# Linear attention into a SoLU block: three of nine chunks take their attention with tokens on partitions

## The chip, the cores and the metric

The kernel runs on one core of a Trainium2 chip. Its engines work beside each other, each through its own instructions in order: TensorE (PE in the profile, its weight loads PEld), VectorE (DVE), ScalarE (ACT), GpSimd (POOL) and SyncE (SP, which here only issues DMAs). They wait for each other by semaphores. The metric is device time in microseconds; lower is better.

## The reference

Inputs are q, k and v of shape (8, 8, 576, 64): batch, heads, tokens, head size; g_norm (64), w_in (512 x 1024), w_out (1024 x 512) and g_ln (1024), all float32.

```
kv  = einsum('bhsd,bhse->bhde', k, v)
out = einsum('bhsd,bhde->bhse', q, kv)
rms = sqrt(mean(out*out, axis=-1) + 1e-6)
x   = (out / rms * g_norm), heads side by side      # 4608 tokens x 512
h   = x @ w_in                                       # 4608 x 1024
sm  = exp(h - max) / (sum(exp(h - max)) + 1e-9)
solu = h * sm
ln  = (solu - mean) / sqrt(var + 1e-6) * g_ln
y   = ln @ w_out                                     # 4608 x 512
```

## The kernel before, in words

The 4608 tokens are nine chunks of 512. Chunks 0 to 7 are one batch each, its tokens j = 0 to 7 of every group of nine; chunk 8 is the ninth token of every group, from all batches. For a chunk c the pieces of work have names, and the prediction uses them:

- `k`, `v`, `q`: loads, converted to bfloat16 on the way, issued on POOL's queue (L265), apart from the first k and v, which SP and ACT issue. `wi`, `wo`: loads of w_in and w_out.
- `kv` (L310): k^T v of a batch; `kc`: its copies to SBUF.
- `qt`/`qc`: q turned by TensorE and copied, in chunks 0 to 4. `qx` (L366): q turned by a DMA, in chunks 5 to 8. `ql`: the ninth tokens put together for chunk 8.
- `o` (L403): q kv, with the features of two heads on partitions and 512 tokens along the row, two banks a piece.
- `sq` (L416, ACT): squares; `s` (L431, TensorE): a matmul with a block matrix of 1/64, which gives the mean of squares of every head to all its 64 partitions; `ln` and `ex` (L435, L439, ACT): its inverse root; `x` (L449, DVE): x = o times that times g_norm.
- `h` (L489 for chunks 0 to 2, L498 for 3 to 8): x w_in; `e` (ACT): exp; `u` (DVE, L523 and L528): h times exp; `r`: squares of u with their sums; in chunks 0 to 2 `g` and `z` add up on POOL and TensorE. `t` (L553): u turned by a DMA that SP issues, in chunks 3 to 8.
- `st`, `rs`: the statistics of the LayerNorm; `a` (L678): u w_out, in halves of four matmuls; `b` (L693, L695): the scaling by the inverse deviation; `d` (L703): the store.
- `wm` (L661), `wc` (L664): the mean of g_ln * w_out over the rows, by TensorE, and w_out centred by it, by DVE. `warm`: matmuls of zeros.
- `gate` (L339): a copy on POOL of one element of the last q, for which all DMA turns wait: no turn starts before the last load has landed.

Nothing is scheduled at run time. `ORDER` is a table with all pieces in one list; the program issues them in that order, and so every engine's order of work, the choice of engine where there is one (`b0.0/act`) and the buffer (`@S0`) are written there. The buffers are slots, of which P (two PSUM banks each, three slots) and S (one bank, two) pace TensorE: a piece that takes a slot waits until the readers of the one before are done. M, L, rst, osq, lss and ob are slots in SBUF. A piece at the head of an engine that waits holds up all that stands behind it there.

```
SLOTS = {"P": 3, "S": 2, "L": 8, "M": 13, "osq": 4, "lss": 3, "rst": 4, "ob": 7}
```

Of the kernel before, what the change touches and what calls it, by code (L numbers as in the profile page):

```python
# [8 lines left out]
FP32 = mybir.dt.float32  # L9
# [15 lines left out]
QUADRANTS = ()  # L25

# [36 lines left out]
WARM = (13, 6, 2, 1)  # L63
# [15 lines left out]
r1.0/pool@L6 qc2.1/dve e1.1@M10 h1.4+@P2 o2.0@P0 sq2.00@osq0 h1.4 sq2.01@osq1 g1.1 h1.5+ h1.5 e1.2@M11 u1.1 u1.2
s2.00@S1 s2.01@S0 ln2.00@lss0 ln2.01@lss1 h1.6+@P1 h1.6 h1.7+ h1.7 a0.20@S1 e1.3@M6 ex2.00@rst0 u1.3 ex2.01@rst1  # L80
o2.1@P2 a0.21 a0.30@S0 sq2.10@osq1 sq2.11@osq0 b0.2/act@ob0 x2.00@M9 x2.01 s2.10@P1 a0.31 s2.11@S1 ln2.10@lss1
ex2.10@rst1 ln2.11@lss0 b0.3/dve@ob2 ex2.11@rst0 qt3.0@P0 qc3.0/dve@M10 kv3@P1 kc3.1/act x2.10 a1.00@S0 a1.01
qt3.1@S1 v6 x2.11 r1.1/pool r1.2/act r1.3/act qc3.1/dve h2.0@P2 h2.1 h2.2@P0 kc3.0/dve e2.0@M1 u2.0@L4 g1.2 g1.3
g2.0@M6 kc3.2/act h2.3 e2.1@M11 u2.1 q6@M12 z1@S1 g2.1 o3.0@P2 sq3.00@osq0 sq3.01@osq1 r2.0/act@L6 r2.1/pool h2.4@P1
y1 st1 rs1 b1.0/dve@ob3 h2.5 h2.6@P0 h2.7 e2.2@M11 u2.2 g2.2 e2.3@M9 a1.10@S1 a1.11 a1.20@S0 u2.3 qt4.0@P1
b1.1/act@ob4 s3.00@S1 g2.3 s3.01@P0 qc4.0/dve@M9 a1.21 b1.2/dve@ob5 r2.2/act r2.3/pool k7@L1 kv4@P1 kc4.1/dve
ln3.00@lss0 ln3.01@lss1 ex3.00@rst0 ex3.01@rst1 x3.00@M11 x3.01 kc4.2/act ql2/pool o3.1@P0 sq3.10@osq1 z2@S1
a1.30@S0 y2 st2 ql5/act v7 q7@M6 gate@L6 s3.10@P2 sq3.11@osq0 ln3.10@lss1 ex3.10@rst1 kc4.0/dve a1.31 x3.10 d0.1/sp
d0.2/sp s3.11@S1 ln3.11@lss0 b1.3/dve@ob0 o4.0@P1 sq4.00@osq0 a2.00@P2 a2.01 ex3.11@rst0 s4.00@S1 a2.10@S0 rs2 x3.11
h3.00@P0 b2.0/dve@ob1 sq4.01@osq1 s4.01@P2 ln4.00@lss0 ex4.00@rst0 ln4.01@lss0 qt4.1@S1 qc4.1/dve x4.00@M2  # L90
ex4.01@rst1 x4.01 h3.01 h3.10@P2 h3.11 e3.0@M10 u3.0@L5 e3.1@M8 u3.1 a2.11 b2.1/act@ob6 kv5@P1 kc5.1/dve r3.0/dve
r3.1/dve o4.1@P0 sq4.10@osq1 d0.3/pool sq4.11@osq0 a2.20@S1 kc5.0/act a2.21 kc5.2/act s4.10@S0 ln4.10@lss0 s4.11@P2
ln4.11@lss1 ex4.10@rst1 ex4.11@rst0 h3.20@P1 h3.21 x4.10 x4.11 e3.2@M8 u3.2 h3.30@P2 h3.31 h4.00@P0 h4.01 h4.10@P1
e3.3@M11 u3.3 r3.2/act t3.0 qx5@M10 ql0/dve e4.0@M9 u4.0@L3 h4.11 e4.1@M0 a2.30@S0 d1.0/pool b2.2/act@ob3 o5.0@P2
sq5.00@osq0 a2.31 sq5.01@osq1 o5.1@P0 sq5.10@osq2 s5.00@S1 u4.1 b2.3/dve@ob2 h4.20@P1 qx6@M1 t3.1 t3.2 ln5.00@lss1
t3.3 t4.0@L4 r3.3/dve st3 sq5.11@osq0 d1.1/sp d1.2/sp d1.3/sp s5.01@S0 d2.0/pool ln5.01@lss0 ex5.00@rst0 x5.00@M11
ex5.01@rst1 s5.10@S1 ln5.10@lss1 x5.01 t4.1 h4.21 a3.00@S0 a3.01 e4.2@M10 u4.2 t4.2 ex5.10@rst1 s5.11@S1 ln5.11@lss0
qx7@M5 x5.10 h4.30@P2 ex5.11@rst0 h4.31 e4.3@M2 a3.10@S1 d2.1/sp x5.11 d2.2/pool kv6@P1 kc6.2/dve a3.11 r4.0/act
h5.00@P0 kc6.0/act kc6.1/dve o6.0@P1 u4.3 rs3 b3.0/dve@ob4 b3.1/act@ob3 sq6.00@osq0 sq6.01@osq2 r4.1/dve h5.01
e5.0@M9 h5.10@P2 s6.00@S0 s6.01@S1 ln6.00@lss0 ln6.01@lss1 ex6.00@rst0 ex6.01@rst1 u5.0@L2 x6.00@M0 x6.01 h5.11  # L100
e5.1@M8 u5.1 a3.20@S0 a3.21 b3.2/dve@ob0 a3.30@S1 r4.2/act r4.3/act o6.1@P1 sq6.10@osq2 kv7@P0 kc7.1/dve a3.31
kc7.0/dve h5.20@P2 h5.21 sq6.11@osq0 b3.3/act@ob5 kc7.2/act st4 d2.3/sp d3.0/sp e5.2@M2 ql4/dve u5.2 s6.10@S1
s6.11@S0 h5.30@P0 h5.31 ln6.10@lss1 ex6.10@rst1 x6.10 ln6.11@lss0 e5.3@M11 a4.00@S1 t4.3 ex6.11@rst1 x6.11 a4.01
a4.10@S0 t5.0@L6 rs4 b4.0/act@ob4 a4.11 b4.1/dve@ob2 o7.0@P2 sq7.00@osq0 sq7.01@osq2 o7.1@P1 a4.20@S1 s7.00@S0 a4.21
# [20 lines left out]
def kernel(  # L125
# [16 lines left out]
    nc = tc.nc  # L142
# [39 lines left out]
    g_cols = big.tile([128, NF + 1], FP32, name="g_cols")  # L182

# [261 lines left out]
    def x_mul(i):  # L445
        c, hf, z = i
        if (hf, z) == (0, 0):
# [210 lines left out]
    def w_mean():  # L658
        t = T["mean"] = bank("mean")
        for f in range(NF):  # L660
            nc.tensor.matmul(t[:, 0], T["g_mean"][:, f, :], T["w_out", f // 4][:, f % 4, :], start=(f == 0), stop=(f == NF - 1))  # L661
# [98 lines left out]
```

## Time and profile before

| | |
|---|---|
| median of 3 runs | 184.74 us (183.53 to 185.95) |
| the profiled execution | 184.59 us |
| span of its instructions | 182.8 us |
| granted TensorE clock, mean | 0.971 |
| busy PE / DVE / ACT / POOL | 167.0 / 123.0 / 136.0 / 61.1 us |
| read from HBM, written to it | 32.51 MB, 9.44 MB |
| DMA queues, share of 16 engines | software (POOL's) 58.1%, hardware (SP's) 36.8% |

Busy times are of one profiled execution. The mean duration of a matmul there (379 ns for 512 columns) counts its whole way through the array; matmuls overlap, and in the chain they follow each other at 0.216 us. The page cuts the span in 40 slices with the busy share in tenths.

### The profile page before, as it was taken

Reading aid. Unit: us, or ns where it says so; the run is one execution under the profiler, and the core shown is the slowest. Engines: PE = TensorE matmul, PEld = TensorE weight load, DVE = VectorE, ACT = ScalarE, POOL = GpSimd, SP = SyncE. Lnnn points to the kernel's source line nnn. Section 1 sums busy time; section 2 is a strip of 40 time slices with the busy share of each in tenths; the row PEclk is TensorE's granted clock in tenths of the full one; section 3 lists DMA queues with packets and bytes.
Section 4 is the critical chain, followed back from the end, with each engine's and each line's share of the span. In section 5 each row is a group of like instructions: output and inputs, shape, how many; then the busy total and the mean of one; then the engine's idle time right before and its main releaser. Section 6 shows DMA issues by size and latency. Waiting matters only on the chain.

```text
span 182.8 us, 4297 instructions
## 1 busy us (share of the span) xinstructions
PE 167.0 (91%) x1719; PEld 82.0 (45%) x1739; DVE 123.0 (67%) x230; ACT 136.0 (74%) x249; POOL 61.1 (33%) x77
## 2 busy tenths in 40 slices
PE   7697977899999999999949999999999999999991
PEld 2342446445455556445413444544444444444450
DVE  1327586866594778678855769757986989765841
ACT  2349765979897878979856999997994787957350
POOL 7851696723695997001310010300000111211020
PEclk9979996999999999999996999999999999999999
DMA  5999999999999999996899999893254999837655
GB/s 172 248 206 280 338 208 209 205 208 212 253 207 232 208 207 208 207 208 105 233 177 221 240 227 227 237 185 71 77 105 71 251 237 209 225 117 157 130 199 203
DMA packets 53591, 36.19 MB, mean 198 GB/s; under 512 B 35580, under 2 KB 48644, under 8 KB 53572
## 3 DMA queue, kind: packets, MB, share of 16 engines
q0 software_dynamic: 15696, 21.17, 58.1%
q1 hardware_dynamic: 37460, 13.90, 36.8%
q10 hardware_dynamic: 416, 0.85, 1.4%
q8 instruction: 13, 0.21, 0.4%
q14 instruction: 6, 0.05, 0.1%
HBM read 32.51 MB, written 9.44 MB: 229 GB/s over the span
## 4 chain that ended last, share of the span: by engine, by line
PE 80%; DMA 8%; DVE 4%; ACT 3%; issue 3%; ACTq 0%; POOLq 0%
PE ps_S L678 27%; PE ps_P L498 21%; PE ps_P L489 11%; PE ps_P L678 6%; DMA sb_M<-sb_M 4%; DMA sb_M<-in_q_dram 4%; PE ps_P L403 3%; PE ps_S L431 3%; PE ps_P L310 3%; DVE sb_M L449 2%; PE ps_S L355 2%; PE ps_P L204 2%; PE ps_S L607 1%; DVE w_out_sb L664 1%; PE ps_P L431 1%
## 5 line engine op out<-in xcount | busy, mean ns | idle before, releaser
L678 PE MATMUL ps_S<-w_out_sb,sb_L 128*128 128x512 bf16 x220 | 54.4, 379 | 1.1 <-issue 0.8
L498 PE MATMUL ps_P<-w_in_sb,sb_M 128*128 128x512 bf16 x190 | 45.2, 385 | 0.2
L678 PEld LDWEIGHTS <-sb_L 128*128 128x128 bf16 x280 | 26.4, 98 | 31.4 <-issue 1.2
L528 DVE SCALAR_TENSOR_TENSOR sb_L<-ps_P,sb_M 128x1024 bf16<-128x1024 f32 x24 | 29.3, 1223 | 11.4 <-ACT sb_M L515 10.9
L703 POOL DMA_DIRECT2D out_dram<-sb_ob x17 | 10.5, 617 | 78.9 <-ACT sb_ob L693 31.2
L449 DVE SCALAR_TENSOR_TENSOR sb_M<-ps_P,g_cols,sb_rst 128x512 bf16<-128x512 f32 x36 | 27.0, 788 | 8.6 <-ACT sb_rst L439 7.4
L515 ACT ACTIVATE sb_M<-ps_P 128x1024 f32<-128x1024 f32 x24 | 24.5, 1022 | 6.9 <-PE ps_P L498 6.7
L498 PEld LDWEIGHTS <-sb_M 128*128 128x128 bf16 x192 | 18.9, 99 | 23.2 <-issue 1.8
L416 ACT ACTIVATE sb_osq<-ps_P 128x512 bf16<-128x512 f32 x36 | 20.0, 595 | 4.7 <-PE ps_P L403 4.6
L489 PE MATMUL ps_P<-sb_M,w_in_sb 128*128 128x512 bf16 x93 | 22.0, 379 | 0.4 <-issue 0.2
L523 DVE TENSOR_TENSOR sb_L<-ps_P,sb_M 128x1024 bf16<-128x1024 f32 x12 | 14.7, 1224 | 8.8 <-ACT sb_M L508 8.6
L439 ACT ACTIVATE sb_rst<-sb_lss 128x512 f32<-128x512 f32 x32 | 19.3, 631 | 0.4
L559 POOL TENSOR_TENSOR sb_M<-sb_M 128x512 bf16<-128x512 f32 x12 | 15.3, 1276 | 4.1 <-issue 2.2
L508 ACT ACTIVATE sb_M<-ps_P 128x1024 f32<-128x1024 f32 x12 | 12.3, 1023 | 4.5 <-PE ps_P L489 4.5
L548 DVE SCALAR_TENSOR_TENSOR sb_M<-sb_L 128x1024 bf16<-128x1024 bf16 x13 | 15.5, 1218 | 0.0
L695 DVE TENSOR_SCALAR sb_ob<-ps_S,rstd 128x512 f32<-128x512 f32 x15 | 11.2, 748 | 6.3 <-PE ps_S L678 5.4
L435 ACT ACTIVATE sb_lss<-ps_S 128x512 f32<-128x512 f32 x23 | 13.4, 594 | 2.0 <-PE ps_S L431 1.9
L489 PEld LDWEIGHTS <-w_in_sb 128*128 128x128 bf16 x96 | 9.0, 97 | 11.5 <-issue 1.8
L693 ACT ACTIVATE sb_ob<-ps_S,rstd 128x512 f32<-128x512 f32 (+1 forms) x15 | 10.1, 671 | 3.7 <-issue 1.8
L546 ACT ACTIVATE sb_M<-sb_L 128x1024 bf16<-128x1024 bf16 x11 | 11.6, 1053 | 1.3 <-DVE sb_L L528 1.3
L431 PE MATMUL ps_S<-sb_osq,head_mean 128*128 128x512 bf16 x26 | 9.9, 407 | 1.3 <-ACT sb_osq L416 1.2
L678 PE MATMUL ps_P<-w_out_sb,sb_L 128*128 128x512 bf16 x47 | 11.0, 379 | 0.1
(85 smaller groups left out, 178.8 us busy)
## 6 DMA issues: line engine op xcount, KB each, us to landing
out_dram<-sb_ob SPq DMA_DIRECT2D x17, 256.0 KB, 3.9
out_dram<-sb_ob POOLq DMA_DIRECT2D x17, 256.0 KB, 4.1
sb_L<-in_k_dram POOLq DMA_DIRECT2D x6, 576.0 KB, 16.4
sb_L<-in_v_dram POOLq DMA_DIRECT2D x6, 576.0 KB, 18.5
sb_M<-in_q_dram POOLq DMA_DIRECT2D x6, 576.0 KB, 17.3
sb_L<-in_moe_w_out_dram POOLq DMA_DIRECT2D x2, 1024.0 KB, 15.5
sb_M<-in_q_dram POOLq DMA_DIRECT2D x4, 288.0 KB, 11.1
w_in_sb<-in_moe_w_in_dram POOLq DMA_DIRECT2D x2, 512.0 KB, 11.1
```

Of the source, the lines that this page charges most:

```text
L416: nc.scalar.activation(out=t[:, :], in_=T["o", c, hf][:, z], func=AF.Square)
L431: nc.tensor.matmul(t[:, 0], head_mean[:, :], T["osq", i][:, :], start=True, stop=True)
L439: nc.scalar.activation(out=t[:, :], in_=T["lss", i][:, :], func=AF.Exp, scale=-0.5)
L449: nc.vector.scalar_tensor_tensor(out=T["x", c][:, pairs_of(c, hf), :, z], in0=T["o", c, hf][:, z].rearrange("p (n q) -> p n q", n=2), scal ...
L489: nc.tensor.matmul(t[:, f % 2], w_in_sb[:, dt, f * 128:(f + 1) * 128], T["x", c][:, dt].rearrange("p q z -> p (q z)"), start=(dt == 0), st ...
L498: nc.tensor.matmul(T["h", c, m][:, half], T["x", c][:, dt].rearrange("p q z -> p (q z)")[:, m * 128:(m + 1) * 128], w_in_sb[:, dt, half * ...
L515: nc.scalar.activation(out=t.rearrange("p a b -> p (a b)"), in_=T["h", c, m].rearrange("p a b -> p (a b)"), func=AF.Exp, accum_out=T["zsum ...
L523: nc.vector.tensor_tensor(out=flat(T["u", c][:, 2 * p:2 * p + 2, :]), in0=flat(T["h", c, p]), in1=flat(T["e", c, p]), op=MUL)
L528: nc.vector.scalar_tensor_tensor(out=T["un", c][:, m, :], in0=T["h", c, m].rearrange("p a b -> p (a b)"), scalar=1.0, in1=T["e", c, m].rea ...
L548: nc.vector.scalar_tensor_tensor(out=unused, in0=src, scalar=1.0, in1=src, op0=MUL, op1=MUL, accum_out=by)
L559: nc.gpsimd.tensor_tensor(out=T["es", c][:, n, :], in0=e[:, 0, :], in1=e[:, 1, :], op=ADD)
L678: nc.tensor.matmul(T["acc", c, m][:, 0], T["u", c][:, f, m * 128:(m + 1) * 128], w_out_sb[:, f, :], start=(f == 0), stop=(f == NF - 1))
```

## The change

In chunks 6, 7 and 8 the way from q to x is another one:

- `o` (o_rows): the parts of turned q are the weights and kv moves through, 64 columns at a time, so that o comes out with 128 tokens on partitions and all 512 features along the row: 32 matmuls a piece, two pieces a chunk.
- `oc`: o is copied to SBUF as float32, on ACT or DVE. `sq`: squares of 1024 elements a partition, on ACT or POOL. `vd`: DVE adds up each head's 64. `vl`: two short ACT operations make the inverse root. `vg`: POOL makes a tile of 16 x 64 from it and g_norm. `x`: DVE multiplies, in two operations.
- `xt`: four DMA turns a chunk, issued by SP, bring x to features on partitions, as `h` needs it.

So twelve each of `sq`, `s`, `ln`, `ex` and `x` go. The tokens of a tile are now two rows j with 64 groups each, and the store of these chunks writes in that order. The statistics of chunks 0 to 5 stay as they are.

Beside that, w_out's mean is made in two halves as the halves of w_out come, and copied to SBUF (`mc`, on ACT), from where `wc` reads it; g_norm is also loaded to all partitions; there are 39 matmuls of zeros in eleven places for 22 in four; and `ORDER` is new as a whole: among other things the identity is made ahead of the first load on POOL, kv6 stands ahead of o5.0 on TensorE, and the stores d0.1 to d1.3 are all issued by SP.

```diff
+ROWS_OF_X = (6, 7, 8)
-WARM = (13, 6, 2, 1)
+WARM = (11, 6, 4, 3, 2, 2, 2, 5, 1, 1, 2)
 ORDER = """
...
+        if ROWS_OF_X:
+            nc.sync.dma_start(g_rep[:, :], g_norm[None, :].to_broadcast([128, D]))
...
+    def o_rows(c, hf):
+        t = T["o", c, hf] = bank(("o", c, hf))
+        o = t.rearrange("p x (m n r e) -> p x m n r e", m=2, n=2, r=2)
+        for mm in range(2):
+            for n2 in range(2):
+                for hh in range(2):
+                    for x in range(2):
+                        for jj in range(2):
+                            n, j = 2 * n2 + x, 2 * (2 * hf + mm) + jj
+                            at = (9 if c < B else 8) * n + j
+                            half = at % 2
+                            nc.tensor.matmul(
+                                o[64 * jj:64 * jj + 64, x, mm, n2, hh, :],
+                                T["qT", c][64 * half:64 * half + 64, at // 2, 64 * hh:64 * hh + 64],
+                                kv_of(c if c < B else j, n, hh ^ half)[64 * half:64 * half + 64],
+                                start=True, stop=True,
+                            )
+    def o_out(c, hf, engine):
+        t = T["os", c, hf] = room(("os", c, hf), [128, 2, 512], FP32)
+        copy(engine, t.rearrange("p x i -> p (x i)"), T["o", c, hf].rearrange("p x i -> p (x i)"))
+    def o_rows_sq(c, hf, engine):
+        t = T["oq", c, hf] = room(("oq", c, hf), [128, 1024], BF16)
...
+            nc.scalar.activation(out=t[:, :], in_=src, func=AF.Square)
...
+            nc.gpsimd.tensor_tensor(out=t[:, :], in0=src, in1=src, op=MUL)
+    def o_rows_sum(c, hf):
...
+        nc.vector.tensor_reduce(
+            out=T["ms", c, hf][:, :], in_=T["oq", c, hf].rearrange("p (i e) -> p i e", e=D), op=ADD, axis=mybir.AxisListType.X
+        )
+    def o_rows_scale(c, hf):
+        t = T["rg", c, hf] = room(("rg", c, hf), [128, 16, D], FP32)
+        nc.gpsimd.tensor_tensor(
+            out=t[:, :, :], in0=T["rr", c, hf][:, :, None].to_broadcast([128, 16, D]),
+            in1=g_rep[:, None, :].to_broadcast([128, 16, D]), op=MUL,
+        )
+    def x_rows(c, hf):
...
+        for x in range(2):
+            nc.vector.tensor_tensor(
+                out=T["xr", c][:, 2 * hf:2 * hf + 2].rearrange("p m (n x) i -> p x m n i", x=2)[:, x],
+                in0=T["os", c, hf][:, x].rearrange("p (m n i) -> p m n i", m=2, n=2),
+                in1=T["rg", c, hf].rearrange("p (x m n r) e -> p x m n (r e)", x=2, m=2, n=2)[:, x], op=MUL,
+            )
+    def x_turn(c, m):
...
+        nc.sync.dma_start_transpose(T["x", c][:, m], T["xr", c][:, m].rearrange("p n i -> p (n i)"))
...
+    def mean_copy():
+        t = T["mean_sb"] = room("mean_sb", [128, d_model], FP32)
+        nc.scalar.copy(t[:, :], T["mean"][:, 0])
     def w_center(f):
...
-            in1=T["mean"][:, 0], op0=MUL, op1=SUB,
+            in1=T["mean_sb"][:, :], op0=MUL, op1=SUB,
...
+    for half in range(2):
+        plan.add(f"wm{half}", "pe", lambda half=half: w_mean(half), [f"wo{half}", "gm"] + ["wm0"] * half,
+                 [] if half else [("A", "mean")], ["g_mean", ("w_out", half)] + ["mean"] * half)
+    plan.add("mc", "act", mean_copy, ["wm1"], [("rst", "mean_sb")], ["mean"])
```

On TensorE the new table has, around the first DMA turn of q, this order (before, then after; slots left out):

```
h4.00 h4.01 h4.10 h4.11 a2.30 o5.0 a2.31 o5.1 s5.00 h4.20 ... kv6 a3.11 h5.00 o6.0
a2.20 h4.20 h4.21 a2.21 h4.30 o5.0 h4.31 a2.30 s5.00 s5.01 a2.31 a3.00 o5.1 o6.0
```

and SP issues behind the gate

```
t3.0 qx5 qx6 t3.1 t3.2 t3.3 t4.0 d1.1 d1.2 d1.3 t4.1 t4.2 qx7 d2.1 d2.3 d3.0 t4.3 t5.0 t5.1 ...
t3.0 qx5 qx6 t3.1 t3.2 t3.3 qx7 t4.0 t4.1 d2.2 d2.3 t4.2 t4.3 qx8 t5.0 xt6.0 xt6.1 d3.0 xt6.2 d3.2 t5.1 xt6.3 xt7.0 ...
```

More of the change, by code (lines that the diff above doesn't have):

```diff
@@ L85 @@
[L85 to L104, printed above, removed]
@@ L561 @@
     for c in range(NC):
-        xs = [[f"x{c}.{hf}{z}" for z in range(2)] for hf in range(2)]
+        xs = [[f"x{c}.{hf}{z}" for z in range(2)] for hf in range(2)] if c not in ROWS_OF_X else None
         if c in FEATURES_UP:
@@ L655, with w_mean @@
         plan.add(f"rs{c}", "act", lambda c=c: rstd(c), [f"st{c}"])
[L658 to L661, printed above, removed]
+    def w_mean(half):
+        if half == 0:
+            T["mean"] = bank("mean")
+        for f in range(4 * half, 4 * half + 4):
+            nc.tensor.matmul(
+                T["mean"][:, 0], T["g_mean"][:, f, :], T["w_out", half][:, f % 4, :], start=(f == 0), stop=(f == NF - 1)
+            )
+    def mean_copy():
+        t = T["mean_sb"] = room("mean_sb", [128, d_model], FP32)
+        nc.scalar.copy(t[:, :], T["mean"][:, 0])
     def w_center(f):
```

136 lines of the change are left out of this document (96 added, 40 removed).

## The prediction

> **What bounds the kernel now.** I read the page first (busy shares, slices, chain), then the chain in order of time, then busy time by stretch.
>
> ```profile
> PE 167.0 (91%) x1719; PEld 82.0 (45%) x1739; DVE 123.0 (67%) x230; ACT 136.0 (74%) x249; POOL 61.1 (33%) x77
> PE   7697977899999999999949999999999999999991
> DMA  5999999999999999996899999893254999837655
> PE 80%; DMA 8%; DVE 4%; ACT 3%; issue 3%; ACTq 0%; POOLq 0%
> ```
>
> TensorE is the bound: 91% busy and 80% of the chain. It is thin in two places, the first eight slices and the slice with the 4, in the middle. The DMA engines are full for the first 18 slices, the loads. The chain in order of time shows the middle and the end:
>
> ```profile
> 25.98 1.51 DVE w_out_sb L664 x3
> ...
> 37.50 1.02 PE ps_P L489 x4
> ...
> 69.56 0.71 PE ps_P L310 x72
> ...
> 88.14 7.47 DMA sb_M<-sb_M
> ...
> 95.66 0.41 PE ps_P L403 x8
> ...
> 137.52 7.77 PE ps_P L498 x36
> ...
> 178.90 0.48 DVE sb_ob L695
> ```
>
> The DMA at 88.14 is the first turn of q by DMA (qx5); o5.0 at 95.66 waits for it. From there to 178.90 it is TensorE almost alone, at 7.77/36 = 0.216 us for a 512-column matmul. Then 3.9 us of scaling and storing to the end of the span. Busy time by stretch:
>
> ```profile
> 37.50:93.20 55.70, 55.00 (x745) 27.91 (x751) 39.36 (x62) 47.17 (x84) 26.93 (x26) 1.00 1.13 203
> 95.00:100.00 5.00, 4.18 (x26) 1.59 (x28) 2.32 (x7) 2.70 (x5) 0.00 (x0) 0.72 1.11 221
> 95.66:178.90 83.24, 82.41 (x611) 38.38 (x620) 60.67 (x121) 64.96 (x129) 8.42 (x14) 0.98 0.80 177
> ```
>
> The columns are PE, PEld, DVE, ACT, POOL busy, granted clock, DMA share, GB/s. Both long stretches are 99% TensorE. The timeline has the gap in brackets, ahead of o5.0:
>
> ```profile
> 95.66 0.41 PE L403 MATMUL ps_P<-sb_M,kvd 64*64 64x256 bf16 x8 [2.47 <-DMA sb_M<-sb_M]
> ```
>
> It costs 2.5 us, and another 1.4 (28% of 5 us) because the clock after it is 0.72. So the time is: the date of o5.0, plus TensorE's work behind it with its small waits, plus the tail. I work the change out in those three terms.
>
> **Date of o5.0: the loads.** The gate before the turns waits for the last load.
>
> ```profile
> 42.18 1.30 SPq L703 DMA_DIRECT2D out_dram<-sb_ob  x2
> L265 POOL DMA_DIRECT2D sb_L<-in_v_dram x1: 760/760/760, 32.1 to 32.1; - x1
> DMA to landing us min/median/max: 14.8/14.8/14.8
> L265 POOL DMA_DIRECT2D sb_M<-in_q_dram x1: 770/770/770, 32.8 to 32.8; - x1
> DMA to landing us min/median/max: 18.2/18.2/18.2
> L265 POOL DMA_DIRECT2D sb_L<-in_k_dram x1: 803/803/803, 69.5 to 69.5; - x1
> DMA to landing us min/median/max: 10.7/10.7/10.7
> L265 POOL DMA_DIRECT2D sb_M<-in_q_dram x1: 740/740/740, 72.3 to 72.3; - x1
> DMA to landing us min/median/max: 13.6/13.6/13.6
> 85.99 0.57 POOL L339 COPY sb_L<-sb_M 1x1 bf16<-1x1 bf16 x1 [12.97 <-ACT sb_lss L435]
> 86.51 1.84 POOL L703 DMA_DIRECT2D out_dram<-sb_ob  x3
> 86.59 1.37 SPq L553 DMA_TRANSPOSE sb_L<-sb_L  x1
> L366 SPq DMA_TRANSPOSE sb_M<-sb_M x3: 2779/2938/5446, 88.1 to 107.7; - x3
> sb_L<-sb_L SPq DMA_TRANSPOSE x24, 3.3
> ```
>
> k7 lands at 80.2 and q7, two loads on, at 85.9: 2.85 us a load. v3 lands at 46.9 and q3 at 51.0, 4.1 apart, with two stores going out between: 0.63 us a store. Before, three stores (d0.0 to d0.2) go out among the loads. In the new order nine do: d0.3 and d1.0 to d1.3 move to SP's queue, which has nothing else until the gate, and d2.0 stands ahead of the gate on POOL. Six more at 0.63 are 3.8 us; between 2 (if the last ones come too late to matter) and 4.5. Making the identity ahead of the first load costs 0.5 (0 to 0.9, the time that it takes on POOL). The gate falls at 90.3. From gate to landed qx5 took 9.6 us with three stores ahead (86.51); now one is there. t3.0's issue 1.37 and a turn of q without company give 7: 2.9 us of issue, the median, in place of 5.4, and the 2.0 by which qx5's landing (7.47) followed its issue (5.45), after some 0.7 for the gate and semaphores. I take 8, so qx5 lands at **98.3** (96.5 to 99.5).
>
> TensorE itself: the new order does kv6 and three halves of h4 ahead of o5.0 and a2.30 behind it, 0.71 + 3 x 0.86 - 0.86 + a 0.2 statistics matmul moved = 2.7 more than the 55.7 row. The start (37.50, h1.0+) comes out alike. o0.0 stands behind the second kv and the squares behind three copies on ACT, which makes the first h some 2 us later. In the other direction, o1.0 no longer waits for a copy of kv that stands on DVE behind the centrings of w_out (25.98), which I count as 2 us too. The centrings now read the mean from a copy in SBUF (one copy on ACT, by L435's size 0.6), so they share the unknown of DVE beside POOL below; eight of 0.74, held up by 0 to 1 each. The 17 extra zero runs (39 for 22) lie in waits there, 3.7 us at 0.216 if they did not. I take 37.5, between 35.5 and 40. kv4 and kv5 now come within 1 us of their loads' landing: 1 us of waits. TensorE arrives at 37.5 + 55.7 + 2.7 + 1.0 = 96.9. The loads decide, by little: **o5.0 at 98.3, 2.6 later than now**. A quicker start would gain nothing.
>
> **Work behind o5.0.** Rows that price the parts:
>
> ```profile
> L431 PE MATMUL ps_S<-sb_osq,head_mean 128*128 128x512 bf16 x26 | 9.9, 407 | 1.3 <-ACT sb_osq L416 1.2
> L403 PE MATMUL ps_P<-sb_M,kvd 64*64 64x64 bf16 x64 | 0.7, 194 | 0.0
> L416 ACT ACTIVATE sb_osq<-ps_P 128x512 bf16<-128x512 f32 x36 | 20.0, 595 | 4.7 <-PE ps_P L403 4.6
> L435 ACT ACTIVATE sb_lss<-ps_S 128x512 f32<-128x512 f32 x23 | 13.4, 594 | 2.0 <-PE ps_S L431 1.9
> L439 ACT ACTIVATE sb_rst<-sb_lss 128x512 f32<-128x512 f32 x32 | 19.3, 631 | 0.4
> L449 DVE SCALAR_TENSOR_TENSOR sb_M<-ps_P,g_cols,sb_rst 128x512 bf16<-128x512 f32 x36 | 27.0, 788 | 8.6 <-ACT sb_rst L439 7.4 <-ACT sb_rst L443 1.1
> L508 ACT ACTIVATE sb_M<-ps_P 128x1024 f32<-128x1024 f32 x12 | 12.3, 1023 | 4.5 <-PE ps_P L489 4.5
> L523 DVE TENSOR_TENSOR sb_L<-ps_P,sb_M 128x1024 bf16<-128x1024 f32 x12 | 14.7, 1224 | 8.8 <-ACT sb_M L508 8.6
> L548 DVE SCALAR_TENSOR_TENSOR sb_M<-sb_L 128x1024 bf16<-128x1024 bf16 x13 | 15.5, 1218 | 0.0
> L559 POOL TENSOR_TENSOR sb_M<-sb_M 128x512 bf16<-128x512 f32 x12 | 15.3, 1276 | 4.1 <-issue 2.2 <-ACT sb_M L508 1.8
> L540 POOL TENSOR_TENSOR sb_L<-sb_L 128x1024 bf16<-128x1024 bf16 x5 | 9.5, 1895 | 0.0
> ```
>
> TensorE: twelve statistics matmuls go, 12 x 0.216 = 2.6. The 192 small matmuls that make o by rows cost 0.7/64 = 0.011 each, 2.1; those they replace took 4 x 0.41 (95.66) + 0.7: nothing much. Counted out, 83 halves of four matmuls at 0.864 (h and a), eight o at 0.41, four statistics at 0.216 and kv7 at 0.71 (69.56) remain behind o5.0, **76.6**, where before 85 halves, eight o, sixteen statistics and two kv make 81.6. Those 81.6 took 83.24, so 1.6 of small waits, the low clock among them; I keep them.
>
> ACT loses 12 x (0.595 + 0.594 + 0.631) = 21.8 and gains five copies (1.02), two squares (1.05) and 24 short ones (0.2): 12 less. DVE loses 12 x 0.788 = 9.5 and gains one copy 1.2, six sums over 1024 elements (0.7 to 1.2, I take 1.1 by L548) and twelve products of 512 (0.6 by half of L548 to 0.79; 0.67): 6.4 more, in a stretch where it has 60.7 of 83.2. POOL, busy 8.4 there, gains four squares and six scalings of 1024 elements, each 1.9 (L540) to 2.55 (twice L559): 19 to 26. The stores of chunks 6 to 8 write the same bytes in rows of 512 floats; I give that nothing, and the new small load of g_norm nothing. SP gains twelve turns of half L553's 1.37 issue, 8 us, in a queue that issues a turn or a store about half of that time.
>
> The new chain from o to x: copy 1.1, square 1 to 2.5, sum 1.1, Ln and Exp 0.4, scaling 1.9 to 2.5, two products 1.3, turn 3 (3.3 is the median of turns twice as large): 10 to 12 us. From o6.1 to h6.00 TensorE has 15 us of other work, for chunk 7 21, for chunk 8 26. So it is covered by itself, but ACT, DVE and POOL serve in order; what waits there is a5, h6 and the P banks that u on DVE frees. This is the unknown cost: DVE's squares (r), products and the small statistics of the LayerNorm take both operands from SBUF, and POOL's new instructions read SBUF beside them. No such pair is in this trace: when POOL worked (20 to 70 us), DVE's operations had one operand in PSUM. Those pairs cost nothing (L523 holds 1.22 throughout). The lower end is 0. The upper end: some 18 such steps of DVE (4 squares, 6 pairs of products, 8 small ones), each finding POOL at work 60% of the time and waiting for half an operation, 1.1, are 12; TensorE's banked work hides 3: 9. I take 3, nearer to the rows that show nothing.
>
> Sum: 98.3 + 76.6 + 1.6 + 3.0 + 3.9 = 183.4 of span, against 182.8; the profiled execution took 184.59 for its span, 1.8 more, so **185.2**. Its own time is 0.15 under the median of 184.74, so the two compare directly.
>
> On collisions of DVE and POOL the Trainium skill (SBUF — State Buffer, Who interferes with whom) speaks against the change: an instruction of VectorE with two SBUF inputs and one of GpSimd that reads SBUF share a read port, and whichever comes second blocks until the first is through. No pair here shows it. By it the 3.0 would be the upper end.
>
> On the gap, the skill (TensorE: Matmul & The Clock Gate, What's actually happening) gives about 3.4 us of idleness before the clock falls. The row above shows 0.72 after 2.5 us, so the trace does not bear that out. By the page, 1.4 of the 1.6 would go.
>
> **Rivals.** (1) *DVE and POOL block each other* where chunks 6 to 8 overlap (x6.0 to x8.0): the 9 in place of 3 gives 191. It decides as soon as one of the four small statistics steps waits for whole POOL operations, since u behind it holds TensorE's banks. For it: POOL's 19 to 26 us in about 36, DVE near 85%. Against: no row. (2) *The stores do not delay the loads and nothing collides*: qx5 lands as now, o5.0 at 95.7, 95.7 + 78.2 + 3.9 + 1.8 = 179.6. For it: the stores are on another queue than the loads. Against: the 4.1 between v3 and q3. (3) *The change does not bring x in time*: SP's queue holds t5.1 and the turns of x in one order, and h6 waits for a turn behind another's wait; two such waits of a turn's 3 us make 188. Against: the 15 us of cover.
>
> **How the numbers follow.** Forecast 0.45 (its own range 182 to 188), (1) 0.27, (2) 0.17, (3) 0.11. The range, 180.5 to 192, takes in (3) and most of (1), and of (2) its upper part. 2% is about what a measurement can tell: faster is under 181.0, slower over 188.4. Faster 0.15, most of (2); slower 0.32, most of (1), a quarter of (3) and the edge of the forecast; within, 0.53, the rest.
>
> **What would show it.** The gate near 90 and o5.0 near 98 with TensorE idle before it by 1 to 3 us; statistics matmuls 24 for 36; behind o5.0 TensorE busy about 77 us. If DVE's r and the products in chunks 6 to 8 last longer than 1.22 and 0.7, or POOL's scalings scatter, (1) holds. The forecast is wrong if o5.0 moves by over 2 us from 98, or TensorE waits over 8 us behind it.

## The result, and the profile after

The changed kernel takes 226.5 us (median; 223.0 to 230.0), the kernel before 185.0 beside it. Its four times form two groups, 223.0 and 223.3, 229.6 and 230.0, and every ratio, here and below, leaves out times more than 1.5% above the fastest of their kernel. The ratio is 1.207, with an interval of 1.193 to 1.221, so the change costs 38 us. The forecast was 185.2, its range 180.5 to 192.0, with 0.32 on slower. The profiled execution of the changed kernel has a span of 221.2 us, 38.4 more than before. Its page, busy time, TensorE's and the DMA engines' slices (5.5 us each) and the shares of the chain:

```profile
span 221.2 us, 4551 instructions
...
PE   7299986999149798799999997998999999029700
...
DMA  6999999999920799999699989266979999985361
...
PE 43%; DMA 22%; issue 9%; DVE 9%; ACT 7%; POOL 6%; SPq 1%; ACTq 0%; POOLq 0%; DVEq 0%
```

TensorE's share of the chain fell from 80 to 43%. Its row has two holes that were not there before: the digits 1 4 (55 to 66 us), with the DMA slices 2 0 just behind them, and the 0 2 near the end. Busy time in four stretches (columns: PE, PEld, DVE, ACT, POOL, granted clock, DMA share, GB/s):

```profile
55.00:63.00 8.00, 0.97 (x5) 0.24 (x3) 0.19 (x1) 1.64 (x4) 0.00 (x0) 0.75 0.98 186
63.00:78.00 15.00, 12.80 (x276) 7.76 (x277) 10.28 (x20) 8.30 (x13) 8.86 (x7) 0.79 0.38 77
116.36:182.00 65.64, 62.43 (x549) 29.18 (x549) 56.90 (x98) 46.95 (x96) 24.39 (x20) 1.00 0.87 176
182.00:221.20 39.20, 17.60 (x78) 8.04 (x76) 8.00 (x16) 9.30 (x20) 2.78 (x4) 0.76 0.78 116
```

In the middle, where the new statistics and turns are, TensorE is busy for 95% of the time. The loss lies ahead of it and behind it. **The first hole** in the timeline, by engine (POOL, DVE, PE; in brackets the idle time ahead of an instruction and what ended it):

```profile
49.86 0.65 POOL L807 DMA_DIRECT2D out_dram<-sb_ob  x1
...
67.98 3.75 POOL L630 TENSOR_TENSOR sb_L<-sb_L 128x1024 bf16<-128x1024 bf16 x2 [14.96 <-PE ps_P L314]
71.67 0.79 POOL L269 DMA_DIRECT2D sb_L<-in_k_dram  x1
...
62.81 0.75 DVE L795 TENSOR_SCALAR sb_ob<-ps_S,rstd 128x512 f32<-128x512 f32 x1 [7.99 <-DMA out_dram<-sb_ob]
...
63.61 0.61 PE L435 MATMUL ps_S<-sb_osq,head_mean 128*128 128x512 bf16 x1 [7.64 <-DVE sb_ob L795]
...
116.30 0.41 PE L407 MATMUL ps_P<-sb_M,kvd 64*64 64x256 bf16 x8
```

The store at 49.86 is d0.0. In the kernel before it goes out on SP's queue; the change puts it on POOL's, behind the loads issued there. Its landing, and that of the two loads issued just ahead of it (v4, q4), in two answers on their lines:

```profile
L807 POOL DMA_DIRECT2D out_dram<-sb_ob x1: 647/647/647, 49.9 to 49.9; - x1
...
DMA to landing us min/median/max: 12.9/12.9/12.9
...
DMA to landing us min/median/max: 18.2/19.1/20.1
```

q4, issued at 41.9, lands at 62.0; d0.0 lands 0.7 us later, at 62.7. b0.2 on VectorE writes the same slot of sb_ob (ob0), waits 8 us for it, and TensorE behind it 7.6. After that POOL's r1.1 waits 15 us: the squares of chunk 1 now have slot L2, which k3 and v3 hold until kv3's matmuls (L314). The load of k5 stands behind r1.1 on POOL and is issued at 71.67; before, at 38.70. That is the empty stretch of the DMA engines, and o5.0 starts at 116.30 in place of 95.66, 20.6 us late. Behind it the kernel takes 104.9 us in place of 87.1; that is the rest of the 38.

**The second hole.** The chain in order of time; then the answer on the stores' line, of those issued from 180 to 183 us (POOL's three are d6.0, d6.1 and d6.3, SP's is d6.2; the landing times are of all four); then the first DMA turn behind d6.2 on SP's queue, and all 24 turns of u in the kernel before:

```profile
182.36 14.36 DMA out_dram<-sb_ob
...
200.23 17.23 DMA out_dram<-sb_ob
```

```profile
L807 POOL DMA_DIRECT2D out_dram<-sb_ob x3: 798/818/854, 180.7 to 182.7; - x3
...
DMA to landing us min/median/max: 9.8/15.3/15.7
```

```profile
L643 SPq DMA_TRANSPOSE sb_L<-sb_L x1: 9314/9314/9314, 184.2 to 184.2; - x1
```

```profile
L553 SPq DMA_TRANSPOSE sb_L<-sb_L x24: 1231/1330/2152, 86.6 to 170.9; - x24
```

The stores' line for the late stores of the kernel before (issued from 159 to 180 us):

```profile
L703 POOL DMA_DIRECT2D out_dram<-sb_ob x5: 611/620/622, 159.6 to 175.7; - x5
...
DMA to landing us min/median/max: 2.4/2.9/3.4
```

With the same bytes, a store takes 10 to 16 us in place of 2.4 to 3.4. The issue of a turn of u takes 9.31 us, where none took more than 2.15 before, and TensorE waits for that turn (9.32 us) and in the same stretch, behind ScalarE, for a slot of sb_ob (9.16).

### The profile page after: what moved, and what is told of

Same layout as the page of the kernel before. It is cut to its first block, busy times and chain, and to the rows that moved or that the text cites. A ratio compares the mean times of both kernels' runs of the same rounds, so it can differ in the third digit from the quotient of the medians.

```text
span 221.2 us, 4551 instructions
## 1 busy us (share of the span) xinstructions
PE 175.6 (79%) x1840; PEld 85.8 (39%) x1840; DVE 138.7 (63%) x235; ACT 123.2 (56%) x233; POOL 83.3 (38%) x85
## 4 chain that ended last, share of the span: by engine, by line
PE 43%; DMA 22%; issue 9%; DVE 9%; ACT 7%; POOL 6%; SPq 1%; ACTq 0%; POOLq 0%; DVEq 0%
DMA out_dram<-sb_ob 19%; PE ps_S L778 14%; PE ps_P L587 12%; PE ps_P L578 6%; DMA sb_M<-in_q_dram 4%; POOL sb_M L649 2%; DVE w_out_sb L761 2%; PE ps_P L314 2%; ACT sb_ob L793 2%; DVE q_last L176 2%; DVE sb_L L618 2%; PE ps_S L697 2%; PE ps_P L206 1%; PE ps_S L359 1%; PE ps_P L407 1%
## 5 line engine op out<-in xcount | busy, mean ns | idle before, releaser
L778 PE MATMUL ps_S<-w_out_sb,sb_L 128*128 128x512 bf16 x248 | 61.9, 392 | 13.3 <-ACT sb_ob L793 9.6
L793 ACT ACTIVATE sb_ob<-ps_S,rstd 128x512 f32<-128x512 f32 (+1 forms) x16 | 10.5, 670 | 34.9 <-DMA out_dram<-sb_ob 28.4
L578 PE MATMUL ps_P<-sb_M,w_in_sb 128*128 128x512 bf16 x96 | 23.9, 390 | 0.0
L453 DVE SCALAR_TENSOR_TENSOR sb_M<-ps_P,g_cols,sb_rst 128x512 bf16<-128x512 f32 x24 | 17.9, 786 | 3.5 <-ACT sb_rst L443 2.1
L630 POOL TENSOR_TENSOR sb_L<-sb_L 128x1024 bf16<-128x1024 bf16 x7 | 13.7, 1966 | 15.7 <-PE ps_P L314 15.0
L420 ACT ACTIVATE sb_osq<-ps_P 128x512 bf16<-128x512 f32 x24 | 13.4, 594 | 8.1 <-PE ps_P L407 8.0
L638 DVE SCALAR_TENSOR_TENSOR sb_M<-sb_L 128x1024 bf16<-128x1024 bf16 x13 | 17.2, 1335 | 0.0
L443 ACT ACTIVATE sb_rst<-sb_lss 128x512 f32<-128x512 f32 x20 | 12.3, 629 | 8.0 <-DVE sb_M L453 7.7
L503 POOL TENSOR_TENSOR sb_M<-rr,g_rep 128x1024 f32<-128x1024 f32 x6 | 11.8, 1970 | 12.7 <-ACT rr L499 9.3
L206 PE MATMUL ps_P<-zeros 128*128 128x512 bf16 x38 | 12.7, 469 | 1.2 <-DVE zeros L189 1.2
L435 PE MATMUL ps_S<-sb_osq,head_mean 128*128 128x512 bf16 x16 | 6.1, 393 | 9.2 <-DVE sb_ob L795 7.6
## 6 DMA issues: line engine op xcount, KB each, us to landing
sb_L<-in_moe_w_out_dram POOLq DMA_DIRECT2D x2, 1024.0 KB, 17.4
```

The lines of the kernel that those rows point to most:

```text
L206: nc.tensor.matmul(t[:, 0], zeros[:, 0:128], zeros[:, :], start=True, stop=True)
L453: nc.vector.scalar_tensor_tensor(out=T["x", c][:, pairs_of(c, hf), :, z], in0=T["o", c, hf][:, z].rearrange("p (n q) -> p n q", n=2), scal ...
L578: nc.tensor.matmul(t[:, f % 2], w_in_sb[:, dt, f * 128:(f + 1) * 128], T["x", c][:, dt].rearrange("p q z -> p (q z)"), start=(dt == 0), st ...
L630: nc.gpsimd.tensor_tensor(out=dst, in0=src, in1=src, op=MUL)
L638: nc.vector.scalar_tensor_tensor(out=unused, in0=src, scalar=1.0, in1=src, op0=MUL, op1=MUL, accum_out=by)
L778: nc.tensor.matmul(T["acc", c, m][:, 0], T["u", c][:, f, m * 128:(m + 1) * 128], w_out_sb[:, f, :], start=(f == 0), stop=(f == NF - 1))
```

## The experiments

The theory after the two traces: (A) the form of the stores of chunks 6 and 7, an outermost dimension of 2, makes each slow; (B) d0.0 behind the loads, then the slot of r1, starve TensorE and the loads. The rival is the forecast's own: VectorE and GpSimd hold each other up. Ratios are to the kernel before, run beside each; gains in us are taken from the ratios, the times given are medians.

**The stores in two DMAs each (e1_split).**

```
+ if c in ROWS_OF_X and c < B:
+     for j in range(2):
+         start(rows_of(c, m)[j, :, cols], T[key][64 * j:64 * j + 64, :])
```

> Only the stores of chunks 6 and 7 change: each goes out as two DMAs of 64 rows of 512 floats (one for each half of the partitions) in place of one with an outermost dimension of 2. Theory A (the form of the late stores confines each to few DMA engines, and slots of sb_ob, the turns on SP's queue and the last stores wait behind them): in the chain of the changed kernel the two waits for out_dram<-sb_ob at the end are 14.36 and 17.23 us, together 31.6; two stores of the usual kind took 2.5 to 5 us each there, so about 24 us go: 202 us (198 to 207), and the stores of chunks 6 and 7 land within 6 us of their issue. Rival (VectorE and GpSimd hold each other up through the middle, which I gave a chance of 0.27): the end is late because its work is late, the form costs nothing, 226 us (222 to 230).

Measured: 207.2 us, ratio 1.124 (1.117 to 1.132). 15 us of the 38 go. The answer on the stores' line from 183 to 198 us:

```profile
L810 POOL DMA_DIRECT2D out_dram<-sb_ob x10: 527/527/560, 183.6 to 197.6; - x10
...
DMA to landing us min/median/max: 2.6/3.8/4.9
```

Twice as many DMAs, each in a quarter of the time (the medians 3.8 and 15.3). The rows of a half store lie as far apart in the output as those of the slow ones, so it is not the addresses that make them slow. A holds. The gain is smaller than the 24 expected: on the pages, ScalarE still waits 9.1 us for slots of sb_ob, where it waited 28.4.

**The form alone, in the kernel before (e5_form).**

```
- return out[c * S:c * S + S, :].rearrange("(p j) d -> p j d", j=9)[:, 2 * m:2 * m + 2]
+ order = "j p" if c in (6, 7) else "p j"
+ rows = out[c * S:c * S + S, :].rearrange(f"(p j) d -> {order} d", j=9)
+ two = slice(2 * m, 2 * m + 2)
+ return rows[two] if c in (6, 7) else rows[:, two]
```

> The kernel before, with one edit: the eight stores of chunks 6 and 7 write in the form of the changed kernel, an outermost dimension of 2 (two blocks of 64 rows), so that rows of these two chunks go to places other than the reference's; bytes, their number and the queues stay. Theory A (this form alone confines a store to few DMA engines): each of the eight takes 8 to 15 us from issue to landing in place of 2.5 to 7, slots of sb_ob and what is queued behind them come late, 200 us (192 to 210). Rival (the form costs something only where the queues are as full as in the changed kernel): 185 us (182 to 188).

Measured: 201.1 us against 183.8, ratio 1.088 (1.079 to 1.098): the form alone costs 16 us in a kernel that has nothing else of the change. The answer on the stores' line from 157 to 185 us, and two answers of the DMA view on the software queue, POOL's: from 163 to 168 us, when only d6.1's packets ran there, and, in the kernel before, from 161 to 162 us with stores of the usual form:

```profile
L706 POOL DMA_DIRECT2D out_dram<-sb_ob x6: 796/796/857, 157.0 to 184.4; - x6
...
DMA to landing us min/median/max: 10.0/13.5/15.6
```

```profile
q0 software_dynamic: 55, 0.22, 11.6%
```

```profile
q0 software_dynamic: 89, 0.30, 79.4%
```

The columns are packets, MB and the share of 16 engines. 0.116 x 16 = 1.9: the store keeps two engines busy. The usual form keeps 0.794 x 16 = 12.7 busy and moves more in 1 us than d6.1 in 5. The chain shows who paid, the turns on SP's queue, where d6.0, of the same form, was issued just ahead of them:

```profile
155.57 16.09 DMA sb_L<-sb_L
...
172.37 10.19 DMA sb_L<-sb_L
```

On this the Trainium skill (DMA: Bandwidth & Descriptors, Why a DMA increments its semaphore by 16 and not by 1) says that a DMA runs on the largest number of engines, up to 16, that divides the slowest dimension (of a size other than 1) of both its patterns. By it a store of 2x64x512 has 2 engines and one of 64x2x512 has 16. The trace agrees: 1.9 engines for the one and 12.7 on average for the other, and the split store's 64 rows land in 3.8 us again.

**d0.0 back on SP's queue (e2_d00sp)**, `d0.0/pool` to `d0.0/sp` in the order.

> Only one word of the order changes: d0.0, the first store of chunk 0, goes to SP's queue in place of GpSimd's, where it stood behind the loads (issued at 49.86, landed at 62.71 us). Theory B: the 7.99 us that VectorE waits for its slot of sb_ob, and the 7.64 us that TensorE waits behind that, go; what follows moves up by as much: 8 us less, 218 us (214 to 221). Rival (the loads, not this wait, set the date of o5.0): the loads still stand behind r1.1, so o5.0 stays at 116 us and the time at 226 us (222 to 230).

Measured: 219.5 us, ratio 1.177 (1.160 to 1.193): 6 us less where 8 were expected, and the interval is wide. The wait of VectorE is gone. d0.0 and d0.1, issued by SP at 44.5 and 45.2 with the same loads in flight, land in

```profile
DMA to landing us min/median/max: 7.1/8.1/9.1
```

so it is the place behind the loads, not the loads themselves, that made it 12.9.

**Both (e3_both).**

> Both edits: the stores of chunks 6 and 7 in two DMAs each, d0.0 on SP's queue. If A and B are separate and add: 226 - 24 - 8 = 194 us (188 to 200). If they are one thing seen twice, the larger alone: 202 us. If the collisions of VectorE and GpSimd are the cause, 222 us or more.

Measured: 195.7 us, ratio 1.059 (1.047 to 1.071). Together they take 27 us off; one by one 15 and 6. They are two things. The traces, one execution each, show why the sum falls short. This is o5.0 in e1_split, in e2_d00sp and here:

```profile
116.75 0.41 PE L407 MATMUL ps_P<-sb_M,kvd 64*64 64x256 bf16 x8
```

```profile
105.07 0.41 PE L407 MATMUL ps_P<-sb_M,kvd 64*64 64x256 bf16 x8
```

```profile
106.27 0.41 PE L407 MATMUL ps_P<-sb_M,kvd 64*64 64x256 bf16 x8
```

d0.0 brings o5.0 forward by 10 to 11 us with or without the other edit. Behind o5.0 the split brings 104.9 us down to 88.9 (205.6 - 116.75), but d0.0 alone leaves 113.6 (218.7 - 105.07): with the slow stores still there, part of what it gains is lost again at the end. Why it grows to 113.6 is not shown.

**The squares of chunk 1 in a slot of their own (e4_l6)**, `r1.0/act@L2` to `r1.0/act@L6` on top of both.

> Both edits, and the squares of chunk 1 (r1.0 to r1.3) in a slot of their own (L6) in place of L2, which the k and v of batch 3 hold until kv3's matmuls: GpSimd's r1.1 waited 14.96 us for it, with the load of k5 behind it. Theory: the load of k5 is issued at about 58 us in place of 71.67, the loads of batches 5 to 7 land about 6 us earlier than with the two edits alone, and o5.0 starts near 103 us (116.36 in the changed kernel): 189 us (185 to 193). Rival (TensorE itself arrives at o5.0 no earlier, or the transfers share what bandwidth there is): the loads land earlier, but the time stays within 2 us of the run with two edits.

Measured: 193.4 us, ratio 1.041 (1.026 to 1.056), 3 us under the run with two edits, though the intervals overlap. In the trace k5 was issued at 55.24, q7 landed at 94.6, and o5.0 starts 4.6 us earlier. The expectation had 189; the loads came, the time only in part. Timeline of TensorE: h1.0+ and o5.0; then its busy time ahead of and behind o5.0:

```profile
41.36 0.59 PE L578 MATMUL ps_P<-sb_M,w_in_sb 128*128 128x512 bf16 x2
...
101.64 0.41 PE L407 MATMUL ps_P<-sb_M,kvd 64*64 64x256 bf16 x8
```

```profile
0.00:101.60 101.60, 90.64 (x1216) 45.70 (x1216) 71.33 (x123) 66.94 (x118) 55.48 (x62) 0.97 1.11 212
101.60:188.80 87.20, 77.93 (x625) 36.65 (x624) 64.93 (x114) 56.30 (x115) 28.54 (x28) 1.00 0.89 187
```

```profile
0.00:95.66 95.66, 84.62 (x1108) 43.63 (x1120) 61.88 (x109) 71.03 (x120) 52.66 (x63) 0.96 1.13 216
95.66:182.80 87.14, 82.41 (x611) 38.38 (x620) 61.16 (x121) 64.96 (x129) 8.42 (x14) 0.98 0.79 178
```

The last pair is the kernel before. Behind o5.0 both spans take 87 us: the changed kernel has 4.5 us less work for TensorE there and 4.5 more idle time. What remains in this execution, 6 us, lies ahead of o5.0: 6.0 us more busy time of TensorE, the idle time alike (11.0). Of that busy time 4.9 are the zero matmuls (12.85 us for 7.96), which e11_warm below takes out without gain. (This execution is the fastest of its kernel; the median is 2.9 us longer. The later runs whose order is the same up to o5.0, e6_sqact, e8_tail and e9_ract, start it at 104.11, 102.63 and 102.58, so one trace does not resolve 2 us here.)

The other runs each take one suspected cause out of this three-edit kernel.

**GpSimd's squares to ScalarE (e6_sqact)**, `sq6.0/pool`, `sq6.1`, `sq7.1` and `sq8.1` to `act`.

> The kernel with three edits (both fixes and L6), and the four squares of chunks 6 to 8 that GpSimd had (sq6.0, sq6.1, sq7.1, sq8.1, 1.89 us each) go to ScalarE. If what is left (193.4 against 184.9) is VectorE and GpSimd holding each other up, 7.6 us of GpSimd's work are gone from the stretch from 112 to 160 us, VectorE's long records there (L638 at a mean of 1597 ns against 1218 in the kernel before) shrink and the time falls by 2 to 4 us: 190 us. If it is VectorE's own amount of work, or ScalarE's, the time stays or rises by up to 2 us: 193 to 195.

Measured: 196.1 us, ratio 1.064 (1.056 to 1.071). Slower, not faster. The wide scatter of r on VectorE stays (min/median/max in ns, first in the three-edit run, then here), with the scalings (vg) still on GpSimd:

```profile
L638 DVE SCALAR_TENSOR_TENSOR sb_M<-sb_L x13: 1208/1219/2532, 88.8 to 170.3; 128x1024 bf16<-128x1024 bf16 x13
```

```profile
L638 DVE SCALAR_TENSOR_TENSOR sb_M<-sb_L x13: 1211/1217/2537, 89.9 to 177.9; 128x1024 bf16<-128x1024 bf16 x13
```

So the squares on GpSimd are not what is left. Why it is slower is not shown; ScalarE is busier, 38.66 us in place of 35.10 from 112 to 160 us. No run takes the scalings off GpSimd.

**Three squares of rows from VectorE to ScalarE (e9_ract)**, `r4.2/dve`, `r4.3`, `r5.2` to `act`.

> The kernel with three edits, and three squares of rows (r4.2, r4.3, r5.2, 1.2 to 2.5 us each on VectorE) on ScalarE in place of VectorE. From 120 to 140 us of the three-edit kernel VectorE was busy for 19.47 of 20 us and TensorE for 17.37; in the kernel before TensorE was busy for 19.90 there. If VectorE's amount of work is what holds TensorE in that stretch: TensorE's idle time there falls by 1.5 to 2.5 us and the time by 1 to 2: 191.5 to 192.5 us. If not, 193.4 or, where ScalarE becomes the bound, up to 195.

Measured: 194.2 us, ratio 1.049 (1.043 to 1.056): no gain.

**The queue at the end (e8_tail)**, `d6.2/sp`, `d7.0`, `d7.2` to `pool`.

> The kernel with three edits, and the stores d6.2, d7.0 and d7.2 on GpSimd's queue in place of SP's, where each is now two DMAs and stands among the turns of chunk 8. The chain of the three-edit kernel has 1.58 us of SP's queue and 3.86 us of out_dram<-sb_ob at 170 us. If the queue and the slots of sb_ob still bind there: 3 us less, 190.4 us (188.5 to 192). If not, 193.4 within 1.

Measured: 193.5 us, ratio 1.053 (1.047 to 1.060): no gain.

**Loads earlier (e7_loads, e10_early)**, first q6, k7 and v7 right behind v6, then v1b, q1b, k2 and v2 right behind k1b as well.

> The kernel with three edits, and on GpSimd's queue the loads q6, k7 and v7 ahead of the work of chunk 2 (right behind v6), since q6 was issued at 75.69 us, 3.2 us before v6 landed. If the date of o5.0 (101.6 us) is still set by the loads: q7 lands at 91 us in place of 94.6, o5.0 starts near 99.5, the time falls by 2: 191.5 us. If TensorE's own work ahead of o5.0 sets it: the loads land earlier and the time stays within 1 us of 193.4.

> The kernel with three edits, and on GpSimd's queue the loads v1b, q1b, k2 and v2 right behind k1b (they were issued from 30.65 to 38.59 us, behind the sums and squares of chunk 0), and q6, k7, v7 right behind v6. In the kernel before, the loads up to q4 landed at 60.28 us, here at 63.86, and q7 at 85.84 against 94.63. If the loads' order on GpSimd's queue is what is left of the late o5.0: q4 lands near 61, q7 near 92, o5.0 starts near 99, and the time is 191 us (189.5 to 192.5). If TensorE's own work ahead of o5.0 sets its date: 193.4 within 1.

Measured: 193.0 us, ratio 1.044 (1.035 to 1.052), and 195.1 us, 1.054 (1.046 to 1.062). q7 itself was issued later (79.24 and 81.39, for 77.95 with three edits) and landed at 95.5 and 96.4: issuing the loads ahead of it earlier did not bring it forward. What the loads share the DMA engines with is the subject of the next run.

**Three stores moved out of the loads (e12_stores)**, on top of e7_loads: `d1.1/sp d1.2/sp d1.3/sp` behind `t3.0 qx5 qx6`, and five slots of sb_ob changed.

> The run before with early loads of q6, k7 and v7 (192.98), with three of the stores that go out among the loads (d1.1, d1.2, d1.3) issued behind the first turns of the gate, and the slots of sb_ob dealt out anew so that nobody waits for them. The forecast put 0.63 us on each store among the loads. If that is right and the loads set the date of o5.0: q7 lands 1.9 us earlier than the 95.49 there, o5.0 starts 2 us earlier, and the time is 191 us. If TensorE's own work sets the date: q7 lands earlier and the time stays at 193 within 1 us. If the stores do not delay the loads: q7 at 95.5.

Measured: 198.9 us, ratio 1.079 (1.071 to 1.086). The loads did as the forecast's price says: q7's landing, first in e7_loads (issue at 79.24), then here (issue at 80.38), and here TensorE's timeline at o5.0:

```profile
DMA to landing us min/median/max: 16.3/16.3/16.3
```

```profile
DMA to landing us min/median/max: 13.0/13.0/13.0
```

```profile
103.12 1.03 PE L587 MATMUL ps_P<-w_in_sb,sb_M 128*128 128x512 bf16 x4
104.08 0.41 PE L407 MATMUL ps_P<-sb_M,kvd 64*64 64x256 bf16 x8
```

79.24 + 16.3 = 95.5; 80.38 + 13.0 = 93.4: 2.1 us for three stores, 0.7 each (0.63 forecast), from one execution of each. But o5.0 follows h4 without a gap: TensorE itself was late. The time is longer; the trace shows stalls near 140 us that the new slots made (b4.2 waited for a store that stood on POOL behind a scaling).

**Fewer zero matmuls (e11_warm)**, ten of the eleven runs at one matmul each.

> The kernel with three edits, and ten of the eleven zero runs at one matmul each (39 zero matmuls become 21, as many as the kernel before has but one). The chain of the three-edit kernel goes through zero matmuls for 2.69 us at 11.48 and 0.43 us at 20.30. If they hold the start up: 1 to 3 us less, 191 us. If they fill idle time and keep the clock up: the same, or up to 2 us more by a lower clock (0.72 to 0.8 in the first 40 us).

Measured: 193.6 us, ratio 1.045 (1.038 to 1.051): no gain. The zero runs lie in waits, and without them the granted clock of the first 41 us is 0.84 in place of 0.92.

**The start as before, alone and with the loads (e13_start, e14_start_loads)**, the first stretch of the order put back, and with it the early loads and the moved stores.

> The kernel with three edits, and the first stretch of the order (up to the last x of chunk 0) as in the kernel before: identity behind the first loads, kv of chunk 0 ahead of the turn of q, copies of kv shared by VectorE and ScalarE, 22 zero matmuls there. If the start is what makes TensorE late: h0 begins near 16.5 us (20.75 in the three-edit run, 16.41 in the kernel before), h1.0+ near 38 (41.36). The loads then land as late as now (q7 at 94 to 95), so that a gap of 1 to 3 us in front of o5.0 comes back and the time falls by 0 to 1.5: 192 to 193.4 us. If the start is not the cause: h1.0+ stays near 41.

> The run with the start of the kernel before, and also q6, k7 and v7 issued right behind v6 and d1.1 to d1.3 behind the first turns of the gate (with the slots of sb_ob dealt so that b4.2 and b4.3 are exchanged). If TensorE's start and the loads stood side by side as bounds of o5.0: o5.0 starts near 98.5 us, and the time is 189 to 191 us. If what is left lies behind o5.0 (VectorE's chain from 120 to 160 us): o5.0 near 98.5 and the time still 192 to 194.

Measured: 194.5 us, ratio 1.044 (1.034 to 1.055), and 195.1 us, 1.062 (1.053 to 1.071). In the second, h0, h1.0+ and o5.0 on TensorE, then the landing of q7 (issued at 76.77):

```profile
19.02 1.89 PE L578 MATMUL ps_P<-sb_M,w_in_sb 128*128 128x512 bf16 x8
...
40.20 0.59 PE L578 MATMUL ps_P<-sb_M,w_in_sb 128*128 128x512 bf16 x2
...
102.87 0.41 PE L407 MATMUL ps_P<-sb_M,kvd 64*64 64x256 bf16 x8
```

```profile
DMA to landing us min/median/max: 13.3/13.3/13.3
```

h0 comes 1.7 us earlier than with three edits (20.75), h1.0+ 1.2, q7 4.6 (90.1), o5.0 not at all. So neither the start nor the loads, nor both together, are what holds o5.0; what does is not found.

## Why the prediction was wrong, point by point

The sum ran: o5.0 at 98.3, 76.6 of work behind it, 1.6 of small waits, 3.0 of collisions, 3.9 of tail.

1. **"The stores of chunks 6 to 8 write the same bytes in rows of 512 floats; I give that nothing."** This step failed: the term was put at nothing without a row behind it, and it is 15 us in the changed kernel (e1_split) and 16 in the kernel before (e5_form), more than any other single edit takes off. I counted bytes and rows and did not look at the order of the dimensions, which had turned from "p j" to "j p". The diff showed it. Chunk 8's stores are not slow: their two dimensions follow each other in one step of nine rows, 128 in all, and in e1_split, where they were not split, they land in 1.7 to 3.4 us.

2. **The date of o5.0: "The gate falls at 90.3 ... qx5 lands at 98.3."** This failed by 18 us. The price of a store among loads came out near (0.7 against 0.63). What I left out is what the store and the slot wait for: I listed the stores that move to SP's queue, not d0.0, which moves the other way, to POOL's; and I took the loads as issued when the queue has room, where one of them now stands behind r1.1 and r1.1 behind slot L2. d0.0 costs 6 us alone (e2_d00sp) and 12 on top of e1_split; the slot about 3 (e4_l6).

3. **"TensorE arrives at 37.5 + 55.7 + 2.7 + 1.0 = 96.9. The loads decide, by little."** This failed too. With both faults mended o5.0 starts at 101.64. h1.0+ came at 41.36, outside the 35.5 to 40 that I allowed, and all of that stands ahead of h0, which starts at 20.75 in place of 16.41: 4.3 us, where I had 2 and took them back later. The loads do not decide: in e12_stores q7 came 2 us earlier, in e14_start_loads 4.6, and o5.0 did not. Only in e6_sqact did o5.0 wait for its turn, 1.31 us.

4. **Work behind o5.0.** 76.6 forecast, 77.9 measured with three edits. Its idle time is 87.2 - 77.9 = 9.3, where waits, collisions and tail were 1.6 + 3.0 + 3.9 = 8.5. This part of the sum held, once the two faults were out; in the changed kernel 104.9 us follow o5.0, not 85.1.

5. **Collisions, rival 1.** The mechanism is there. VectorE's groups after, and the centring of w_out (wc) before:

```profile
L638 DVE SCALAR_TENSOR_TENSOR sb_M<-sb_L 128x1024 bf16<-128x1024 bf16 x13 | 17.2, 1335 | 0.0
L761 DVE SCALAR_TENSOR_TENSOR w_out_sb<-sb_L,g_cols,sb_rst 128x512 bf16<-128x512 f32 x8 | 8.4, 1092 | 0.2 <-ACT sb_rst L758 0.2
```

```profile
L664 DVE SCALAR_TENSOR_TENSOR w_out_sb<-sb_L,g_cols,ps_S 128x512 bf16<-128x512 f32 x8 | 5.6, 742 | 0.1
```

r rose from 1218 to 1335 ns, 13 x 0.117 = 1.5 us in sum; wc, which now has both large operands in SBUF, from 742 to 1092, 8 x 0.35 = 2.8 us, where I had allowed "0 to 1 each". Three copies of q_last, 0.22 us each before, add 5.0; one of them, 3.82 us at 85.92, stands in the chain. Wc is on TensorE's way once: in the three-edit run TensorE waited 1.84 us for it at 37.62. So VectorE's work is some 9 us longer in sum; how much of it reaches the time is not shown. The Trainium skill (SBUF — State Buffer, Who interferes with whom) has such pairs block each other; the rows agree. Rival 1's 191 is no account of the 226, but it may have a part in what is left below.

6. **Rivals 2 and 3.** The stores among the loads do delay them (e12_stores), against rival 2. Turns did come late, with 9.31 us for the issue of one, but behind and beside confined stores and not, as rival 3 had it, behind one another.

7. **Two small sums.** ACT loses 21.8 and gains 12.0, so 9.8 less, not 12 (measured behind o5.0 with three edits: 64.96 - 56.30 = 8.7). Rival 3's two waits of 3 us added to 185.2 make 191, not 188. Neither enters the forecast.

With both faults mended and the slot moved, 193.4 us are left, 4% over the kernel before and just above the range. Of these 7.5 us no run takes any away, and steps of 1 to 2 us are not resolved by intervals of this width. In the fastest trace 6 lie ahead of o5.0: 3.9 up to h1.0+, 2.1 from there to o5.0, where TensorE has 3.8 us more work (58.78 for 55.00). From 120 to 140 us VectorE is busy for 19.5 of 20 us and TensorE for 17.4. Which of these is the cause stays open. No version tried beats the kernel before.

## What to carry to other kernels

When a store's pattern changes, look at its outermost dimension, not only at its bytes: keep 64 or 128 rows there, if need be as two DMAs. When a DMA moves to another queue, ask what stands ahead of it there and who waits for the slot that it frees; when a tile moves to another slot, ask who holds the slot and which loads are queued behind the one that waits. Here TensorE's work behind o5.0 came out near its forecast, and 31 of the 38 us came from two entries of the table and the order of two dimensions.

## What the runs showed of the hardware that was not expected

- A 256 KB store with an outermost dimension of 2 kept 1.9 of 16 engines busy (e5_form, 163 to 168 us) and landed 9.8 to 15.7 us after its issue; one of the usual form, late in the kernel before, 2.4 to 3.4; halves of 64 rows 2.6 to 4.9.
- Turns on SP's queue came late behind and beside such stores: a wait for a turn of 16.09 us stands in the chain of e5_form, where nothing else was changed. One store of this form stood ahead of the turn on SP's queue, three on POOL's; which of them held it is not separated.
- A store issued on POOL's queue 8 us after a load landed 0.7 us after that load, 12.9 us after its issue; on SP's queue, beside the same loads, it took 7.1 to 9.1.
- A copy of 128x256 on VectorE (q_last), 220 ns in the kernel before, took up to 3818 ns in the changed kernel: it ran from 85.9 to 89.7 us, and GpSimd was at work beside it from 80.3 to 89.7.
